# The 64-token rests of an attention and mixer kernel as pairs of 64-row and 64-column matmuls

## Chip, core and metric

The kernel runs on one core of one Trainium2 chip. The core has a matrix engine (TensorE, PE in the profile, with a queue of its own for weight loads, PEld), three engines for elementwise work (VectorE or DVE, ScalarE or ACT, GpSimd or POOL), and SyncE (SP), which here issues most of the DMAs. The engines run side by side and wait for each other by semaphores. The metric is the device time of one execution in microseconds; lower is better.

## The reference

For 8 batches of 576 tokens and 8 heads of 64 columns: heads 0 to 3 attend to the last 32 tokens, heads 4 to 7 to every fourth of the last 128. Then a mixer over tokens and one over channels:

```python
scores = scale * np.matmul(q, k.transpose(0, 1, 3, 2))
mask_plain = (rel >= 0) & (rel < 32)
mask_dil = (rel >= 0) & (rel < 128) & (rel % 4 == 0)
attn = exp(scores - max) / sum              # masked
x = np.matmul(attn, v)                      # [8, 576, 512]
h = np.maximum(xt @ w_tok1, 0.0) @ w_tok2   # xt: x with tokens last, 576 -> 256 -> 576
u = x + h.transpose(0, 2, 1)
h2 = np.maximum(u @ w_ch1, 0.0) @ w_ch2     # 512 -> 1536 -> 512
return u + h2
```

## The kernel before

**Tiles.** 576 tokens are four blocks of 128 and a rest of 64, the tail. The attention output of a batch, `xn`, is [128, 5, 512] in 16-bit floats: slots 0 to 3 hold the four blocks, slot 4 the tail. For columns 0 to 255 (heads 0 to 3) the blocks hold tokens in their natural order, for columns 256 to 511 every fourth token, as the dilated heads use them.

**The tail in three steps.** `values(b, h)` (L605) multiplies the exponentials of the scores with v, one head at a time; the last column of v is 1, so that the sums come with it, and a reciprocal and a product on VectorE normalise all five slots at once. The tail's exponentials lie in `attt`, 320 columns for each head (L147), of which two pieces of 64 are written and the rest is 1.0 (L171). The tail's matmul (L625) reads a window of 128 columns, in which the 64 written ones come first for even and last for odd batches, so all 128 rows of slot 4 get finite values and the real ones stand in rows 0 to 63 or 64 to 127. Heads 4 to 7 need a second such matmul, over v's rows 384 to 447, which are loaded and cast into a tile of their own (`l_vx`, `vt`; "v's middle rows").

`emit_h1(b, jb, half, t)` (L631) gives h1, the hidden layer over tokens: for each half of the columns and each of two blocks `jb` of 128 hidden units, one matmul over slot 4 (L637) with the weight rows 512 to 575 in `w1t[b % 2]`, whose other 64 rows are zero (L179), and four over slots 0 to 3 (L639), summed in one bank of PSUM. `emit_u(b, s, h1)` (L642) gives u; for the tail (s = 4, L659 to L666) two matmuls, 512 wide, with the last 64 columns of w_tok2 inside a window of 128 columns in `w2`, which is padded with 64 columns of zeros on the right (L180), so that the 64 real rows land in the half where `xn` has them; two batches share one tail tile `u16t`. Batch 0 has its own form, `u_half` (L1108).

**Order.** The program's order is written out by hand. For batch 0 it is a straight list (L1009 to L1139). From then on `interleave` (L983) mixes the channel matmuls of batch b (`gen_main`, L920: gp, gt, yp, yx, yw) with steps for batch b + 1 (values, then `mix_steps`, L902: h1, u, transposes) and batch b + 2 (casts and scores), by a time given to each step and a cost that it adds to the clock of the mix. So TensorE's stream is one list, and a step waits there for its inputs.

**PSUM.** `bank("fl", 3, ...)` hands out three banks in a ring to values, h1, u and transposes; a new tenant waits until the bank's last one has been read.

**Forms of matmuls.** Nearly all are 128 rows by 128 columns of weights. The scores of batches 2 to 7 (`scores_twin`, L512) are pairs of 64 rows each, one for each head of a pair, in sets of 20 and 24.

**Loads.** All inputs of later batches go through SyncE's queue in the order of `load_steps` (L226); v in eight pieces: four of 128 tokens for heads 0 to 3, then the tail, two pieces for heads 4 to 7 (`l_vd`) and the middle rows (`l_vx`). GpSimd casts them in the same order (`cast_steps`, L278) and issues the weights' DMAs between its casts (L1038 to L1055).

Of the kernel before, what the change touches and what calls it, by code (L numbers as in the profile page):

```python
# [12 lines left out]
ALU = mybir.AluOpType  # L13
# [19 lines left out]
PST = 256  # L33
PW = 4 * PST
DTL = 512
TW = 320
CBS = (2, 0, 3, 1)
GW = 2 * S

# [29 lines left out]
def kernel(  # L69
# [16 lines left out]
    def fixed(name, shape, dtype=FP16):  # L86
        return sb.tile(shape, dtype, tag=name, bufs=1, name=name)
# [60 lines left out]

    w1n = fixed("w1n", [128, 4, DTOK])
    w1p = fixed("w1p", [128, 4, DTOK])  # L150
    w1t = [fixed(f"w1t{i}", [128, DTOK]) for i in range(2)]
    w2a = fixed("w2", [128, 2, 640])
    w2 = [w2a[:, i] for i in range(2)]
    w2p = [fixed(f"w2p_{i}", [128, 4, 128]) for i in range(2)]
    w3 = [fixed(f"w3_{i}", [128, 4, 512]) for i in range(3)]
# [7 lines left out]
    def emit_fixed():  # L163
        nc.gpsimd.memset(idle, 0.0)
        nc.gpsimd.memset(spread, 0.0)
        nc.vector.memset(qza[64:128, :, 0], 0.0)
        nc.vector.memset(qza[0:64, :, 1], 0.0)
        for a in attp:
            nc.gpsimd.memset(
                a.rearrange("p h (b c) -> p h b c", c=PST)[:, :, :, 128:PST], 0.0)  # L170
        nc.vector.memset(attt, 1.0)  # L171
        for i in range(2):
            nc.gpsimd.memset(vt[i][64:128], 0.0)

    def emit_fixed_late():
        for i in range(2):
            nc.gpsimd.memset(vv[i][:, :, :, 64:65], 1.0)
            nc.gpsimd.memset(vt[i][0:64, :, 64:65], 1.0)
            nc.gpsimd.memset(w1t[i], 0.0)  # L179
        nc.gpsimd.memset(w2a[:, :, S:640], 0.0)  # L180


    l32 = {}
# [19 lines left out]
    def load_v_steps(b):  # L203
        tn = sb.tile([128, 4, 4, D], FP32, tag="l_vn", bufs=1, name=f"l_vn_{b}")
        td = sb.tile([128, 4, 4, D], FP32, tag="l_vd", bufs=1, name=f"l_vd_{b}")
        tx = sb.tile([64, 4, D], FP32, tag="l_vx", bufs=1, name=f"l_vx_{b}")
        t = sb.tile([128, H, D], FP32, tag="l_vt", bufs=1, name=f"l_vt_{b}")
        l32[(b, "vn")], l32[(b, "vd")], l32[(b, "vx")], l32[(b, "vt")] = tn, td, tx, t

        def go(out, in_):  # L210
            return lambda: nc.sync.dma_start(out=out, in_=in_)  # L211

        steps = [go(tn[:, s], v[b, 0:4, 128 * s:128 * s + 128, :].rearrange("h s d -> s h d"))
                 for s in range(4)]
        steps.append(go(t, v[b, :, 448:S, :].rearrange("h s d -> s h d")))
        for h in (0, 2):
            steps.append(go(td[:, h:h + 2].rearrange("m h r d -> m h (r d)"),
                            v[b, 4 + h:6 + h, 0:512, :].rearrange("h (m r) d -> m h (r d)", r=4)))
        steps.append(go(tx, v[b, 4:8, 384:448, :].rearrange("h s d -> s h d")))
        return steps  # L220

    def load_v(b):
# [55 lines left out]
    def cast_steps(b, eng=nc.gpsimd):  # L278
        steps = [lambda: cast_tails_qk(b, eng)]
        for hp in range(4):  # L280
            for nm in ("q", "k"):
                steps.append(lambda nm=nm, hp=hp: cast_qk(b, nm, hp, eng))
        for s in range(4):
            steps.append(lambda s=s: cast_vn(b, s, nc.gpsimd))
        steps.append(lambda: cast_tail_v(b, nc.gpsimd))
        for h in (0, 2):
            steps.append(lambda h=h: cast_vd(b, h, nc.gpsimd))
        steps.append(lambda: cast_vx(b, nc.gpsimd))
        return steps


# [150 lines left out]
        return slice(384 + 64 * x, 512 + 64 * x)  # L442

    def tail_cols(t, hp):
        return t[..., 64:TW].rearrange("p z (x c) -> p z x c", c=128)[:, :, near(hp)[0]:, 0:64]

    def tails_mask(hp):
        return tails_seen[hp // 2][:, :, near(hp)[0]:]
# [155 lines left out]

    def values(b, h):  # L605
        hp, i = h // 2, h % 2
        odd = b % 2
        va = vv[b % 2]
        av = bank("main" if b == 0 and h % 2 else "fl", 3, f"av_{b}_{h}")[:, 0:325].rearrange("p (s c) -> p s c", c=65)
        if hp < 2:  # L610
            a = attp[hp][:, i]
            for s in range(4):
                if s:
                    nc.tensor.matmul(out=av[:, s], lhsT=a[:, PST * (s - 1) + 128:PST * s],
                                     rhs=va[:, s - 1, h, :], start=True, stop=False)
                nc.tensor.matmul(out=av[:, s], lhsT=a[:, PST * s:PST * s + 128],  # L616
                                 rhs=va[:, s, h, :], start=(s == 0), stop=True)
        else:
            a = attd[hp - 2][:, i]
            for r in range(4):  # L620
                nc.tensor.matmul(out=av[:, r], lhsT=a[:, 128 * r:128 * r + 128],  # L621
                                 rhs=va[:, r, h, :], start=True, stop=True)
        c0 = 0 if odd else 64
        for x in near(hp):
            nc.tensor.matmul(out=av[:, 4], lhsT=attt[:, hp, i, c0 + 128 * x:c0 + 128 * x + 128],  # L625
                             rhs=va[:, 4, h, :] if x else vt[b % 2][:, h - 4, :], start=x == near(hp)[0], stop=x == 1)
        rec = sb.tile([128, 5, 1], FP32, tag="rec", bufs=4, name=f"rec_{b}_{h}")
        nc.vector.reciprocal(out=rec[:, :, 0], in_=av[:, :, 64])  # L628
        mult(nc.vector, xn[b][:, :, D * h:D * h + D], av[:, :, 0:64], rec)

    def emit_h1(b, jb, half, t):  # L631
        x = xn[b]
        j = slice(jb, DTOK, 2)
        c = slice(256 * half, 256 * half + 256)
        w = w1p if half else w1n
        p = bank("fl", 3, f"h1p_{b}_{jb}_{half}")[:, 0:256]
        nc.tensor.matmul(out=p, lhsT=w1t[b % 2][:, j], rhs=x[:, 4, c], start=True, stop=False)  # L637
        for s in range(4):
            nc.tensor.matmul(out=p, lhsT=w[:, s, j], rhs=x[:, s, c], start=False, stop=(s == 3))  # L639
        relu(nc.vector if jb and half and b == 0 else nc.scalar, t[:, c], p)  # L640

    def emit_u(b, s, h1):  # L642
        p = bank("fl", 3, f"up_{b}_{s}")
# [12 lines left out]
            else:  # L656
                nc.vector.tensor_tensor(out=u16(b, s), in0=blocks4(p), in1=blocks4(xn[b][:, s]), op=ALU.add)  # L657
        else:
            odd = b % 2  # L659
            c0 = 448 if odd else 512  # L660
            for jb in range(2):
                nc.tensor.matmul(out=p, lhsT=w2[jb][:, c0:c0 + 128], rhs=h1[jb],  # L662
                                 start=(jb == 0), stop=(jb == 1))
            rows = slice(64, 128) if odd else slice(0, 64)
            t = u16t[b // 2]
            nc.vector.tensor_tensor(out=t[rows], in0=blocks4(p[rows]), in1=blocks4(xn[b][rows, 4]), op=ALU.add)  # L666

    def emit_uT(b, cb):
        odd = b % 2
# [232 lines left out]
    def mix_steps(b, t_h1, t_h1b, t_u, t_uT, du=1.0, turn=6.0, gap=2.6):  # L902
        h1 = [sb.tile([128, DM], FP16, tag="h1", bufs=4, name=f"h1_{b}_{jb}") for jb in range(2)]
        steps = []
        for half, at in ((0, t_h1), (1, t_h1b)):
            for jb in range(2):
                steps.append((at + 0.9 * jb, 0.55, lambda jb=jb, half=half: emit_h1(b, jb, half, h1[jb])))
        for i, s in enumerate((4, 0, 1, 2, 3)):
            steps.append((t_u + du * i, 0.44, lambda s=s: emit_u(b, s, h1)))
        if turned(b):  # L910
            for t, tail in ((turn, False), (turn + 1.0, True))[:1 + b % 2]:
                steps.append((t_u + t * du, 0.0, lambda tail=tail: uT_dma(b, tail)))
# [125 lines left out]
    nc.gpsimd.dma_start(out=w1p, in_=moe_w_tok1[0:512, :].rearrange("(m r) j -> m r j", r=4))  # L1038
    for hp in range(2, 4):
        cast_qk(0, "q", hp, nc.gpsimd)  # L1040
    nc.gpsimd.dma_start(out=w1t[0][0:64], in_=moe_w_tok1[512:S, :])
    nc.gpsimd.tensor_copy(out=spread[:, 3:515:4], in_=ident)
    cast_qk(0, "k", 3, nc.gpsimd)
    for s in range(4):
        cast_vn(0, s, nc.gpsimd)
    nc.gpsimd.dma_start(out=w2a[:, :, 0:S], in_=moe_w_tok2.rearrange("(p j) t -> p j t", j=2))
    load_w3(0)
    cast_vd(0, 0, nc.gpsimd)
    cast_vd(0, 2, nc.gpsimd)
    load_w3(1)  # L1050
    cast_vx(0, nc.gpsimd)
    nc.gpsimd.dma_start(out=w1t[1][64:128], in_=moe_w_tok1[512:S, :])
    for jb in range(2):
        nc.gpsimd.tensor_copy(
            out=w2p[jb], in_=w2[jb][:, 0:512].rearrange("p (m r) -> p r m", r=4))  # L1055
# [52 lines left out]
    def u_half(s, half):  # L1108
        p = bank("main" if half else "fl", 3, f"up_0_{s}_{half}")[:, 0:256]
        c = slice(256 * half, 256 * half + 256)  # L1110
        rows = slice(0, 64) if s == 4 else slice(0, 128)
        t = (u16t[0] if s == 4 else u16(0, s))[:, 2 * half:2 * half + 2]
        summed = s in (0, 2)
        if summed:
            nc.tensor.matmul(out=p, lhsT=ident, rhs=xn[0][:, s, c], start=True, stop=False)
        for jb in range(2):
            lhsT = w2p[jb][:, s] if half and s < 4 else w2[jb][:, 128 * s:128 * s + 128]
            nc.tensor.matmul(out=p, lhsT=lhsT, rhs=h1[jb][:, c], start=(jb == 0 and not summed),
                             stop=(jb == 1))
        if summed:  # L1120
            nc.scalar.copy(out=t, in_=blocks4(p))
        else:
            nc.vector.tensor_tensor(out=t[rows], in0=blocks4(p[rows]), in1=blocks4(xn[0][rows, s, c]), op=ALU.add)

    for jb in range(2):
        emit_h1(0, jb, 0, h1[jb])
    for s in (0, 2):
        u_half(s, 0)
    for jb in range(2):
        emit_h1(0, jb, 1, h1[jb])  # L1130
    for s in (4, 1, 3):
        u_half(s, 0)
    for s in (4, 3, 0):
# [126 lines left out]
```

## Time and profile before

| | us |
|---|---|
| median of three runs | 276.93 (275.76 to 277.38) |
| the profiled execution | 275.95 |
| its span, first to last instruction | 274.1 |

The page's first lines give for each engine its busy time, the share of the span and its instructions, and the span in 40 equal slices, each digit the busy share in tenths (9 is 90% or more); PEclk is the clock that TensorE was granted, in tenths:

```
PE 265.5 (97%) x2694; PEld 197.3 (72%) x2694; DVE 168.4 (61%) x340; ACT 148.7 (54%) x291; POOL 159.9 (58%) x216
PE   6899989999999999999999999999999999999994
PEclk9999999999999999999999999999999999999999
```

Rows of a timeline read: start in us from the span's start, duration of the group in us, engine, line of the kernel, operation, output and inputs by the program's names, shape (for TensorE, rows by columns of weights in use, then the moving operand), how many, and in brackets the engine's idle time before and what ended it. Rows of groups give busy us, mean ns of one, and idle time before with what ended most of it. Rows of waits give the total in us, the number, and the longest. A matmul's end is modelled, and matmuls overlap, so their starts tell more than their durations.

### The profile page before, as it was taken

Reading aid. Unit: us, or ns where it says so; the run is one execution under the profiler, and the core shown is the slowest. Engines: PE = TensorE matmul, PEld = TensorE weight load, DVE = VectorE, ACT = ScalarE, POOL = GpSimd, SP = SyncE. Lnnn points to the kernel's source line nnn. Section 1 sums busy time; section 2 is a strip of 40 time slices with the busy share of each in tenths; the row PEclk is TensorE's granted clock in tenths of the full one; section 3 lists DMA queues with packets and bytes.
Section 4 is the critical chain, followed back from the end, with each engine's and each line's share of the span. In section 5 each row is a group of like instructions: output and inputs, shape, how many; then the busy total and the mean of one; then the engine's idle time right before and its main releaser. Section 6 shows DMA issues by size and latency. Waiting matters only on the chain.

```text
span 274.1 us, 6762 instructions
## 1 busy us (share of the span) xinstructions
PE 265.5 (97%) x2694; PEld 197.3 (72%) x2694; DVE 168.4 (61%) x340; ACT 148.7 (54%) x291; POOL 159.9 (58%) x216
## 2 busy tenths in 40 slices
PE   6899989999999999999999999999999999999994
PEld 2787676898676876687776876787776866786673
DVE  6667668676567656595557553875475464961363
ACT  2864675353674655467545666576646565236500
POOL 8871761289868659659974689749970870000000
PEclk9999999999999999999999999999999999999999
DMA  7999999995999799999999899979999040525015
GB/s 220 269 240 231 295 236 207 295 241 150 347 172 219 159 295 198 308 181 240 300 231 214 260 258 255 193 138 330 326 180 152 3 154 2 99 79 149 0 41 153
DMA packets 111471, 54.98 MB, mean 201 GB/s; under 512 B 82736, under 2 KB 107312, under 8 KB 111440
## 3 DMA queue, kind: packets, MB, share of 16 engines
q1 hardware_dynamic: 106784, 49.10, 77.0%
q0 software_dynamic: 2640, 3.94, 8.1%
q10 hardware_dynamic: 2016, 1.51, 1.8%
q8 instruction: 21, 0.34, 0.5%
q14 instruction: 10, 0.08, 0.1%
HBM read 37.59 MB, written 9.44 MB: 172 GB/s over the span
## 4 chain that ended last, share of the span: by engine, by line
PE 89%; DMA 5%; DVE 2%; SPq 1%; ACT 1%; issue 0%; ACTq 0%; POOL 0%
PE gp L941 30%; PE yx L783 13%; PE yw L783 9%; PE h1p L639 5%; PE up L651 4%; PE gt L932 4%; PE yp L969 4%; PE yp L752 4%; PE sc L524 3%; DMA lt<-in_k_dram 3%; DMA l_vx<-in_v_dram 2%; PE h1p L637 1%; PE av L621 1%; SPq L211 1%; PE av L616 1%; PE up L662 1%
## 5 line engine op out<-in xcount | busy, mean ns | idle before, releaser
L109 ACT ACTIVATE gt<-gp 128x512 f16<-128x512 f32 x89 | 53.3, 598 | 49.8 <-PE gp L941 49.5
L783 PEld LDWEIGHTS <-gt 128*128 128x128 f16 x600 | 57.0, 98 | 8.2
L941 PE MATMUL gp<-utd,w 128*128 128x512 f16 x144 | 54.7, 380 | 0.0
L941 PE MATMUL gp<-utm,w 128*128 128x512 f16 x144 | 54.6, 379 | 0.0
L941 PEld LDWEIGHTS <-w 128*128 128x128 f16 x384 | 39.0, 113 | 19.8 <-issue 0.5
L115 POOL TENSOR_TENSOR attp<-attp,const 128x1280 f16<-128x1280 f16 x12 | 31.6, 2637 | 22.1 <-ACT attp L549 22.1
L739 DVE TENSOR_TENSOR gt<-gt 128x768 f16<-128x768 f16 x56 | 32.5, 610 | 12.5 <-ACT gt L109 12.1
L115 DVE TENSOR_TENSOR xn<-av,rec 128x320 f16<-128x320 f32 x64 | 31.5, 492 | 2.2
L115 POOL TENSOR_TENSOR attd<-attd,const 128x1024 f16<-128x1024 f16 x12 | 25.5, 2127 | 5.9 <-issue 5.1
L941 PE MATMUL gp<-uT,w 128*128 128x512 f16 x96 | 25.8, 379 | 0.0
L796 DVE TENSOR_TENSOR o<-yx,u 128x512 f32<-128x512 f32 x22 | 15.2, 691 | 11.6 <-PE yx L783 11.4
L549 ACT ACTIVATE attp<-sc 128x480 f16<-128x480 f32 (+1 forms) x36 | 15.9, 538 | 8.8 <-PE sc L524 8.8
L783 PE MATMUL yx<-w,gt 128*128 128x256 f16 x168 | 20.6, 273 | 0.0
L783 PE MATMUL yx<-wsum_a,gt 128*128 128x256 f16 x168 | 20.6, 273 | 0.0
L657 DVE TENSOR_TENSOR u<-up,xn 128x512 f16<-128x512 f32 x26 | 17.8, 689 | 4.1 <-PE up L651 4.1
L628 DVE RECIPROCAL rec<-av 128x5 f32<-128x5 f32 x64 | 12.3, 192 | 12.7 <-PE av L625 12.6
L105 POOL CAST c_k<-l_k 128x512 f16<-128x512 f32 x29 | 17.6, 615 | 2.2 <-DMA l_k<-in_k_dram 1.1
L666 DVE TENSOR_TENSOR u16t<-up,xn 64x512 f16<-64x512 f32 x7 | 4.8, 690 | 20.8 <-PE up L662 20.8
L105 POOL CAST c_q<-l_q 128x512 f16<-128x512 f32 x26 | 16.3, 633 | 1.9 <-DMA l_q<-in_q_dram 1.2
L870 ACT COPY utd<-utm 128x512 f16<-128x512 f16 x12 | 12.7, 1125 | 8.8 <-DMA u<-utd 4.2
L109 ACT ACTIVATE h<-h1p 128x256 f16<-128x256 f32 x31 | 11.8, 384 | 9.5 <-PE h1p L639 9.1
L806 DVE TENSOR_TENSOR o<-yw,o 128x512 f32<-128x512 f32 x13 | 9.0, 692 | 10.2 <-PE yw L783 10.1
(159 smaller groups left out, 551.3 us busy)
## 6 DMA issues: line engine op xcount, KB each, us to landing
l_q<-in_q_dram SPq DMA_DIRECT2D x15, 512.0 KB, 6.4
l_k<-in_k_dram SPq DMA_DIRECT2D x14, 512.0 KB, 7.1
out_dram<-o SPq DMA_DIRECT2D x12, 512.0 KB, 4.6
l_vn<-in_v_dram SPq DMA_DIRECT2D x32, 128.0 KB, 6.8
l_vd<-in_v_dram SPq DMA_DIRECT2D x16, 256.0 KB, 5.1
w<-in_moe_w_ch_dram POOLq DMA_DIRECT2D x6, 512.0 KB, 7.8
out_dram<-o SPq DMA_DIRECT2D x17, 128.0 KB, 2.6
l_vt<-in_v_dram SPq DMA_DIRECT2D x8, 256.0 KB, 5.5
```

What stands on the lines that cost most here:

```text
L105: eng.tensor_copy(out=out, in_=in_)
L109: nc.scalar.activation(out=out, in_=in_, func=AF.Relu)
L115: eng.tensor_tensor(out=out, in0=x, in1=y, op=ALU.mult)
L549: nc.scalar.activation(out=out, in_=in_, func=AF.Exp, scale=0.125)
L628: nc.vector.reciprocal(out=rec[:, :, 0], in_=av[:, :, 64])
L639: nc.tensor.matmul(out=p, lhsT=w[:, s, j], rhs=x[:, s, c], start=False, stop=(s == 3))
L657: nc.vector.tensor_tensor(out=u16(b, s), in0=blocks4(p), in1=blocks4(xn[b][:, s]), op=ALU.add)
L739: nc.vector.tensor_tensor(out=out, in0=x, in1=y, op=op)
L783: nc.tensor.matmul(out=p, lhsT=gta[:, k0 + mb, r:r + 128], rhs=weights[:, mb, c], start=(first and not mb and (not a or len(parts) > 2)), ...
L796: nc.vector.tensor_tensor(out=o[i][:, :, 256 * j:256 * j + 256].rearrange("p s (x c) -> p s x c", x=2), in0=grid(p), in1=u, op=ALU.add)
L870: nc.scalar.copy(out=natural(uTd[:, cb - 2]), in_=uTm[i][:, cb].rearrange("p r m -> p m r"))
L941: nc.tensor.matmul(out=p, lhsT=w3_block(cb, mb), rhs=uT[(b, cb)][0], start=(i == 0), stop=(i == 3))
```

## The change

- **Tail values.** `attt` shrinks to 128 columns for each head, with the two written pieces side by side and no fill. Each tail matmul becomes two, with the same 64 columns of weights: one writes rows 0 to 63 of slot 4, the other rows 64 to 127, so both halves of `xn`'s slot 4 hold the tail.
- **h1.** `w1t` is one tile now, with the 64 weight rows in both halves. `emit_h1` makes both blocks `jb` of a half: first the two rests, one from rows 0 to 63 and one from rows 64 to 127, then for each block the four other matmuls. Its two steps stand 0.5 apart, with costs 0.54 and 0.43, where it was 0.9 and 0.55.
- **u.** The tail's two 512-wide matmuls become four of 64 columns and 256 wide, in pairs: the left half of the columns to rows 0 to 63 of the bank, the right half to rows 64 to 127. VectorE adds them in two operations. The step's cost goes from 0.44 to 0.22. In batch 0's `u_half` the tail's matmuls take 64 columns of weights instead of 128.
- **Loads.** In each batch v's middle rows are loaded and cast ahead of the two pieces for heads 4 to 7. The second load into `w1t` moves ahead of that of `w2` on GpSimd's queue; the padding of `w2` and the clearing of `w1t` go.

```diff
--- before.py
+++ after.py
@@ -33,7 +33,7 @@
 PST = 256
 PW = 4 * PST
 DTL = 512
-TW = 320
+TW = 128
 CBS = (2, 0, 3, 1)
 GW = 2 * S
 
@@ -148,8 +148,8 @@
 
     w1n = fixed("w1n", [128, 4, DTOK])
     w1p = fixed("w1p", [128, 4, DTOK])
-    w1t = [fixed(f"w1t{i}", [128, DTOK]) for i in range(2)]
-    w2a = fixed("w2", [128, 2, 640])
+    w1t = fixed("w1t", [128, DTOK])
+    w2a = fixed("w2", [128, 2, S])
     w2 = [w2a[:, i] for i in range(2)]
     w2p = [fixed(f"w2p_{i}", [128, 4, 128]) for i in range(2)]
     w3 = [fixed(f"w3_{i}", [128, 4, 512]) for i in range(3)]
@@ -168,7 +168,6 @@
         for a in attp:
             nc.gpsimd.memset(
                 a.rearrange("p h (b c) -> p h b c", c=PST)[:, :, :, 128:PST], 0.0)
-        nc.vector.memset(attt, 1.0)
         for i in range(2):
             nc.gpsimd.memset(vt[i][64:128], 0.0)
 
@@ -176,8 +175,6 @@
         for i in range(2):
             nc.gpsimd.memset(vv[i][:, :, :, 64:65], 1.0)
             nc.gpsimd.memset(vt[i][0:64, :, 64:65], 1.0)
-            nc.gpsimd.memset(w1t[i], 0.0)
-        nc.gpsimd.memset(w2a[:, :, S:640], 0.0)
 
 
     l32 = {}
@@ -213,10 +210,10 @@
         steps = [go(tn[:, s], v[b, 0:4, 128 * s:128 * s + 128, :].rearrange("h s d -> s h d"))
                  for s in range(4)]
         steps.append(go(t, v[b, :, 448:S, :].rearrange("h s d -> s h d")))
+        steps.append(go(tx, v[b, 4:8, 384:448, :].rearrange("h s d -> s h d")))
         for h in (0, 2):
             steps.append(go(td[:, h:h + 2].rearrange("m h r d -> m h (r d)"),
                             v[b, 4 + h:6 + h, 0:512, :].rearrange("h (m r) d -> m h (r d)", r=4)))
-        steps.append(go(tx, v[b, 4:8, 384:448, :].rearrange("h s d -> s h d")))
         return steps
 
     def load_v(b):
@@ -283,9 +280,9 @@
         for s in range(4):
             steps.append(lambda s=s: cast_vn(b, s, nc.gpsimd))
         steps.append(lambda: cast_tail_v(b, nc.gpsimd))
+        steps.append(lambda: cast_vx(b, nc.gpsimd))
         for h in (0, 2):
             steps.append(lambda h=h: cast_vd(b, h, nc.gpsimd))
-        steps.append(lambda: cast_vx(b, nc.gpsimd))
         return steps
 
 
@@ -442,7 +439,7 @@
         return slice(384 + 64 * x, 512 + 64 * x)
 
     def tail_cols(t, hp):
-        return t[..., 64:TW].rearrange("p z (x c) -> p z x c", c=128)[:, :, near(hp)[0]:, 0:64]
+        return t.rearrange("p z (x c) -> p z x c", c=64)[:, :, near(hp)[0]:]
 
     def tails_mask(hp):
         return tails_seen[hp // 2][:, :, near(hp)[0]:]
@@ -604,7 +601,6 @@
 
     def values(b, h):
         hp, i = h // 2, h % 2
-        odd = b % 2
         va = vv[b % 2]
         av = bank("main" if b == 0 and h % 2 else "fl", 3, f"av_{b}_{h}")[:, 0:325].rearrange("p (s c) -> p s c", c=65)
         if hp < 2:
@@ -620,24 +616,28 @@
             for r in range(4):
                 nc.tensor.matmul(out=av[:, r], lhsT=a[:, 128 * r:128 * r + 128],
                                  rhs=va[:, r, h, :], start=True, stop=True)
-        c0 = 0 if odd else 64
         for x in near(hp):
-            nc.tensor.matmul(out=av[:, 4], lhsT=attt[:, hp, i, c0 + 128 * x:c0 + 128 * x + 128],
-                             rhs=va[:, 4, h, :] if x else vt[b % 2][:, h - 4, :], start=x == near(hp)[0], stop=x == 1)
+            for half in range(2):
+                nc.tensor.matmul(out=av[64 * half:64 * half + 64, 4], lhsT=attt[:, hp, i, 64 * x:64 * x + 64],
+                                 rhs=va[:, 4, h, :] if x else vt[b % 2][:, h - 4, :],
+                                 start=x == near(hp)[0], stop=x == 1)
         rec = sb.tile([128, 5, 1], FP32, tag="rec", bufs=4, name=f"rec_{b}_{h}")
         nc.vector.reciprocal(out=rec[:, :, 0], in_=av[:, :, 64])
         mult(nc.vector, xn[b][:, :, D * h:D * h + D], av[:, :, 0:64], rec)
 
-    def emit_h1(b, jb, half, t):
+    def emit_h1(b, half, t):
         x = xn[b]
-        j = slice(jb, DTOK, 2)
         c = slice(256 * half, 256 * half + 256)
         w = w1p if half else w1n
-        p = bank("fl", 3, f"h1p_{b}_{jb}_{half}")[:, 0:256]
-        nc.tensor.matmul(out=p, lhsT=w1t[b % 2][:, j], rhs=x[:, 4, c], start=True, stop=False)
-        for s in range(4):
-            nc.tensor.matmul(out=p, lhsT=w[:, s, j], rhs=x[:, s, c], start=False, stop=(s == 3))
-        relu(nc.vector if jb and half and b == 0 else nc.scalar, t[:, c], p)
+        p = [bank("fl", 3, f"h1p_{b}_{jb}_{half}")[:, 0:256] for jb in range(2)]
+        for jb in range(2):
+            rows = slice(64 * jb, 64 * jb + 64)
+            nc.tensor.matmul(out=p[jb], lhsT=w1t[rows, jb:DTOK:2], rhs=x[rows, 4, c], start=True, stop=False)
+        for jb in range(2):
+            for s in range(4):
+                nc.tensor.matmul(out=p[jb], lhsT=w[:, s, jb:DTOK:2], rhs=x[:, s, c], start=False, stop=(s == 3))
+            relu(nc.vector if jb and half and b == 0 else nc.scalar, t[jb][:, c], p[jb])
+            yield
 
     def emit_u(b, s, h1):
         p = bank("fl", 3, f"up_{b}_{s}")
@@ -656,14 +656,15 @@
             else:
                 nc.vector.tensor_tensor(out=u16(b, s), in0=blocks4(p), in1=blocks4(xn[b][:, s]), op=ALU.add)
         else:
-            odd = b % 2
-            c0 = 448 if odd else 512
+            halves = [(slice(64 * i, 64 * i + 64), slice(256 * i, 256 * i + 256)) for i in range(2)]
             for jb in range(2):
-                nc.tensor.matmul(out=p, lhsT=w2[jb][:, c0:c0 + 128], rhs=h1[jb],
-                                 start=(jb == 0), stop=(jb == 1))
-            rows = slice(64, 128) if odd else slice(0, 64)
-            t = u16t[b // 2]
-            nc.vector.tensor_tensor(out=t[rows], in0=blocks4(p[rows]), in1=blocks4(xn[b][rows, 4]), op=ALU.add)
+                for rows, c in halves:
+                    nc.tensor.matmul(out=p[rows, 0:256], lhsT=w2[jb][:, 512:S], rhs=h1[jb][:, c],
+                                     start=(jb == 0), stop=(jb == 1))
+            t = u16t[b // 2][halves[b % 2][0]]
+            for i, (rows, c) in enumerate(halves):
+                nc.vector.tensor_tensor(out=t[:, 2 * i:2 * i + 2], in0=blocks4(p[rows, 0:256]),
+                                        in1=blocks4(xn[b][rows, 4, c]), op=ALU.add)
 
     def emit_uT(b, cb):
         odd = b % 2
@@ -903,10 +904,11 @@
         h1 = [sb.tile([128, DM], FP16, tag="h1", bufs=4, name=f"h1_{b}_{jb}") for jb in range(2)]
         steps = []
         for half, at in ((0, t_h1), (1, t_h1b)):
+            f = emit_h1(b, half, h1)
             for jb in range(2):
-                steps.append((at + 0.9 * jb, 0.55, lambda jb=jb, half=half: emit_h1(b, jb, half, h1[jb])))
+                steps.append((at + 0.5 * jb, 0.43 + 0.11 * (not jb), lambda f=f: next(f)))
         for i, s in enumerate((4, 0, 1, 2, 3)):
-            steps.append((t_u + du * i, 0.44, lambda s=s: emit_u(b, s, h1)))
+            steps.append((t_u + du * i, 0.44 if s < 4 else 0.22, lambda s=s: emit_u(b, s, h1)))
         if turned(b):
             for t, tail in ((turn, False), (turn + 1.0, True))[:1 + b % 2]:
                 steps.append((t_u + t * du, 0.0, lambda tail=tail: uT_dma(b, tail)))
@@ -1038,18 +1040,18 @@
     nc.gpsimd.dma_start(out=w1p, in_=moe_w_tok1[0:512, :].rearrange("(m r) j -> m r j", r=4))
     for hp in range(2, 4):
         cast_qk(0, "q", hp, nc.gpsimd)
-    nc.gpsimd.dma_start(out=w1t[0][0:64], in_=moe_w_tok1[512:S, :])
+    nc.gpsimd.dma_start(out=w1t[0:64], in_=moe_w_tok1[512:S, :])
     nc.gpsimd.tensor_copy(out=spread[:, 3:515:4], in_=ident)
     cast_qk(0, "k", 3, nc.gpsimd)
     for s in range(4):
         cast_vn(0, s, nc.gpsimd)
-    nc.gpsimd.dma_start(out=w2a[:, :, 0:S], in_=moe_w_tok2.rearrange("(p j) t -> p j t", j=2))
+    nc.gpsimd.dma_start(out=w1t[64:128], in_=moe_w_tok1[512:S, :])
+    nc.gpsimd.dma_start(out=w2a, in_=moe_w_tok2.rearrange("(p j) t -> p j t", j=2))
     load_w3(0)
+    cast_vx(0, nc.gpsimd)
     cast_vd(0, 0, nc.gpsimd)
     cast_vd(0, 2, nc.gpsimd)
     load_w3(1)
-    cast_vx(0, nc.gpsimd)
-    nc.gpsimd.dma_start(out=w1t[1][64:128], in_=moe_w_tok1[512:S, :])
     for jb in range(2):
         nc.gpsimd.tensor_copy(
             out=w2p[jb], in_=w2[jb][:, 0:512].rearrange("p (m r) -> p r m", r=4))
@@ -1109,25 +1111,26 @@
         p = bank("main" if half else "fl", 3, f"up_0_{s}_{half}")[:, 0:256]
         c = slice(256 * half, 256 * half + 256)
         rows = slice(0, 64) if s == 4 else slice(0, 128)
+        p = p[rows]
         t = (u16t[0] if s == 4 else u16(0, s))[:, 2 * half:2 * half + 2]
         summed = s in (0, 2)
         if summed:
             nc.tensor.matmul(out=p, lhsT=ident, rhs=xn[0][:, s, c], start=True, stop=False)
         for jb in range(2):
-            lhsT = w2p[jb][:, s] if half and s < 4 else w2[jb][:, 128 * s:128 * s + 128]
+            lhsT = w2p[jb][:, s] if half and s < 4 else w2[jb][:, 128 * s:128 * s + rows.stop]
             nc.tensor.matmul(out=p, lhsT=lhsT, rhs=h1[jb][:, c], start=(jb == 0 and not summed),
                              stop=(jb == 1))
         if summed:
             nc.scalar.copy(out=t, in_=blocks4(p))
         else:
-            nc.vector.tensor_tensor(out=t[rows], in0=blocks4(p[rows]), in1=blocks4(xn[0][rows, s, c]), op=ALU.add)
-
-    for jb in range(2):
-        emit_h1(0, jb, 0, h1[jb])
+            nc.vector.tensor_tensor(out=t[rows], in0=blocks4(p), in1=blocks4(xn[0][rows, s, c]), op=ALU.add)
+
+    for _ in emit_h1(0, 0, h1):
+        pass
     for s in (0, 2):
         u_half(s, 0)
-    for jb in range(2):
-        emit_h1(0, jb, 1, h1[jb])
+    for _ in emit_h1(0, 1, h1):
+        pass
     for s in (4, 1, 3):
         u_half(s, 0)
     for s in (4, 3, 0):
```

## The prediction

> **What bounds the kernel now.** I read the page's first part, then the busy times by stretches of the span, the waits of TensorE's weight queue (PEld), and last the timeline of TensorE around single steps.
>
> ```profile
> span 274.1 us, 6762 instructions
> ...
> 14.70:27.30 12.60, 11.77 (x162) 9.87 (x159) 8.63 (x26) 6.33 (x16) 5.13 (x10) 1.00 1.16 230
> 42.00:274.10 232.10, 228.43 (x2267) 169.91 (x2264) 140.50 (x281) 123.28 (x238) 132.13 (x158) 1.00 0.84 192
> ...
> PEld L524 <- issue: 2.1, 8, 0.4
> PEld L637 <- DVE xn L115: 1.3, 3, 0.4
> ```
>
> The two rows of stretches, startup and all from 42 us on, give: stretch, its length, then busy time and count of PE, PEld, DVE, ACT and POOL, then the granted clock. From 42 us on PE is busy for 228.4 of 232.1 us at clock 1.00, while DVE, ACT and POOL are busy for 61%, 53% and 57% of it. The two last rows are the longest waits of the weight queue after 42 us; PE's own queue has none there. So in that stretch, which holds the work on batches 1 to 7, the end moves with whatever is added to or taken from PE's stream. In the startup PE is busy for 11.8 of 12.6 us; it also waits for others, and a saving or a cost there can be covered.
>
> What a matmul costs in this stream is not its duration (0.19 to 0.38 us, they overlap) but the step from its start to the next one's start. These are the three places that the change touches, in batch 5 and batch 4:
>
> ```profile
> 165.21 0.20 PE L625 MATMUL av<-vt,attt 128*128 128x65 f16 x1
> 165.24 0.20 PE L625 MATMUL av<-vv,attt 128*128 128x65 f16 x1
> ...
> 165.71 0.27 PE L637 MATMUL h1p<-xn,w1t 128*128 128x256 f16 x1
> 165.82 0.60 PE L639 MATMUL h1p<-xn,w1n 128*128 128x256 f16 x4
> ...
> 139.31 0.59 PE L662 MATMUL up<-h,w 128*128 128x512 f16 x2
> 139.74 0.38 PE L651 MATMUL up<-h,w 128*128 128x256 f16 x2
> ```
>
> A tail value matmul (L625) costs 0.03 us (165.21 to 165.24), the h1 rest (L637) 0.11, the two 512-wide u rests (L662) 0.43 together, 0.22 each, so that a 256-wide one is 0.11.
>
> **The price that decides: leaving the full 128x128 form.** The change makes these matmuls 64 rows or 64 columns wide, between neighbours that stay 128x128. The kernel before has matmuls of 64 rows already, the scores of batches 2 to 7 (L524), in 12 sets. First and last set:
>
> ```profile
> 58.16 0.82 PE L969 MATMUL yp<-w,gt 128*128 128x256 f16 x6
> 58.91 0.65 PE L524 MATMUL sc<-qt,kt 64*128 64x160 f16 x14
> 59.39 0.19 PE L524 MATMUL sc<-tt,kt 64*128 64x64 f16 x2
> 59.42 0.22 PE L524 MATMUL sc<-qt,kt 64*128 64x128 f16 x2
> 59.48 0.19 PE L524 MATMUL sc<-tt,kt 64*128 64x64 f16 x2
> 59.60 0.83 PE L969 MATMUL yp<-w,gt 128*128 128x256 f16 x6
> ...
> 216.42 0.82 PE L783 MATMUL yw<-wsum_b,gt 128*128 128x256 f16 x6
> 217.17 0.62 PE L524 MATMUL sc<-qt,kr 64*128 64x128 f16 x16
> 217.63 0.28 PE L524 MATMUL sc<-tt,kt 64*128 64x64 f16 x8
> 217.84 0.61 PE L783 MATMUL yw<-wsum_b,gt 128*128 128x256 f16 x4
> ```
>
> *Pairs do run side by side:* the two 64-wide matmuls at 59.39 make way for the next group at 59.42, 0.03 us for both, the price of one L625.
>
> *But the set pays on both sides.* Six 256-wide matmuls begin at 58.16 and last 0.82; the last of them (0.27 long) began at 58.71 and should make way at 58.82. The set begins at 58.91: 0.09 lost. Its last pair, at 59.48, should make way at 59.51; the next full matmul begins at 59.60: 0.09 again. The last set says the same: 216.97 + 0.11 = 217.08 against 217.17, and 217.72 + 0.03 = 217.75 against 217.84. With the rounding of the rows I take **0.19 us for each excursion** out of the full form and back, whatever its length. For a set of 20 or 24 matmuls that is little; the change makes excursions of two or four.
>
> The Trainium skill, "TensorEngine Tiling (Array Packing)", section Key Properties, says that changing the tiling mode, other than changing the tile within a mode, drains the TensorE. By that rule, which the two sets bear out for rows, columns pay as well; no run here shows that for columns. With the rule the sum below is +12.7, without it for columns -0.9.
>
> **The change part by part.** Batches 1 to 7 first.
>
> *Tail values:* 8 heads in 7 batches are 56 excursions. Each head's one or two L625 become one or two pairs; by the pair at 59.39 a pair costs 0.03, as the single one did. What is new is the excursion. No trace here has 64-column matmuls; the nearest row is the 64-row set (0.19), from below bounded by nothing, from above by 0.19 plus a weight load that stands open (0.10, below). I take the nearest row: 56 x 0.19 = **+10.6**.
>
> *h1 rests:* 14 halves (7 batches, 2 halves). Two rests of 0.11 become one pair: -0.11; an excursion with 64 rows, which the sets show: +0.19. 14 x 0.08 = **+1.1**.
>
> *u rests:* 7 batches. 0.43 becomes two pairs of 256-wide, 0.22: -0.21; one excursion +0.19. 7 x -0.02 = **-0.1**.
>
> *Batch 0* lies ahead of 27.3 us:
>
> ```profile
> 18.68 0.28 PE L621 MATMUL av<-vv,attd 128*128 128x65 f16 x4
> 19.49 0.19 PE L625 MATMUL av<-vt,attt 128*128 128x65 f16 x1 [0.53 <-POOL vt L105]
> ...
> 16.54 0.62 POOL L105 CAST vv<-l_vd 128x512 f16<-128x512 f32 x1 [0.93 <-DMA l_vd<-in_v_dram]
> 17.39 0.63 POOL L105 CAST vv<-l_vd 128x512 f16<-128x512 f32 x1 [0.23 <-DMA l_vd<-in_v_dram]
> ...
> 19.04 0.40 POOL L105 CAST vt<-l_vx 64x256 f16<-64x256 f32 x1 [0.34 <-DMA l_vx<-in_v_dram]
> ```
>
> Four matmuls of 0.03 from 18.68 should be followed at 18.80; PE waits until 19.49 for v's middle rows. Loaded and cast ahead of the two pieces of v for heads 4 to 7, they come in time, and this 0.7 goes. The two pieces move behind them by one issue on SyncE (0.6) and one cast (0.4): the first is then ready near 17.8, the second near 18.7, still ahead of PE, which needs them at 18.7 and 19.1 at the earliest. What is late next is TensorE itself: three full excursions ahead of 18.68 (a fourth lies partly in the wait for the v tail) bring it to about 19.3, so the 0.7 pays for them and no more. Heads 4 to 7 add 4 x 0.19 and the two h1 halves 2 x 0.08; the two u rests (now 64 columns, otherwise as long) add 2 x 0.19, half of it in PE's waits for DVE and ACT. Sum 0.8 + 0.2 + 0.2 = **+1.1** (0.76 + 0.16 + 0.19). Bounds: -0.5 (the wait goes, no excursion counts) and +2.1 (12 excursions of 0.19 less two pairs of 0.11).
>
> ```profile
> 6.58 0.33 DVE L1033 TENSOR_SCALAR veil<-const 128x416 f16<-128x416 f16 x1 [0.25 <-DMA const<-consts]
> 14.13 0.72 POOL L1046 DMA_DIRECT2D w<-in_moe_w_tok_dram  x1
> 20.10 0.27 PE L637 MATMUL h1p<-xn,w1t 128*128 128x256 f16 x1
> DMA to landing us min/median/max: 5.2/5.9/6.5
> L666 DVE TENSOR_TENSOR u16t<-up,xn 64x512 f16<-64x512 f32 x7 | 4.8, 690 | 20.8 <-PE up L662 20.8
> L1123 DVE TENSOR_TENSOR u16t<-up,xn 64x256 f16<-64x256 f32 x2 | 0.8, 406 | 0.0
> L625 PEld LDWEIGHTS <-attt 128*128 128x128 f16 x96 | 7.2, 97 | 0.6 <-issue 0.6
> ```
>
> *What I cost at nothing.* DVE loses the fill of the tail tile and POOL three clearings, all in the first microseconds; but the first transposes need the identity out of the constants, for whose DMA DVE waits until 6.58 even after the fill. The second load of w1t moves ahead of w2 and the first w3 on POOL's queue, one issue (0.7 or less, as w2's at 14.13) later for each; it would be issued at 14.1 and land 5.2 to 6.5 later (the two loads of w1t), by 20.6; PE needs it at 20.10 + 0.8, near 20.9. If it came late, the wait would be of that size, some 0.3 at most. Each u tail on DVE becomes two additions instead of one, +0.12 seven times, off the path: DVE is busy 61% of the stretch. In later batches the middle rows' load and cast go ahead of those of the other two pieces on SyncE and POOL, which come some 0.6 later; POOL is free 43% of the stretch, and were each late by 0.6, seven times, it would be 4.2. *A wait may be added:* the first step of an h1 half now takes both banks at once, so its second rest asks for a bank one step sooner, and PE's whole stream stands behind it. Three of the 14 halves wait now, 0.4 at most (the L637 row above); if each of them waited as much again, 1.3.
>
> *Sum:* 10.6 + 1.1 - 0.1 + 1.1 = +12.7. The profiled execution took 275.95 (span 274.1 and 1.85 around it), which gives 288.7; the median of the three runs is 276.93, 0.98 above it, which gives **289.6**.
>
> **The rivals.**
> - *Columns are free (not slower).* If only 64-row forms pay, because only they cut the sums that run through the array, values cost nothing, u gains 7 x 0.21 = 1.5, h1 still loses 1.1, batch 0 gains 0.5: -0.9, so **276.0**. For it: no row shows a 64-column price. Against: the price appears on entry and on exit alike, as a change of form would make it. It decides from a column price of 0.04 per excursion down: (1.4 + 0.9) / 63, with 1.4 us being 0.5%.
> - *Nothing pays (faster).* If 0.19 belonged to the score sets and not to the form: -16 x 0.11 - 1.5 - 0.7 = -4.0, **272.9**. Against it stand 12 sets with the same loss after 256-wide and 512-wide neighbours.
> - *The halves don't run side by side.* The pairs in the trace differ in rows, those of the values and u in columns. One after another, heads 0 to 3 cost 0.03 more, heads 4 to 7 0.06: 7 x 0.36 = 2.5, and u's gain of 1.5 goes: **293.6**.
> - *The weight loads stand open.* If each column excursion also waits for one load of weights (0.10, the L625 row of PEld above), 63 x 0.10 and some 0.5 in batch 0: +6.8, **296.4**. For it: after the change of form no load can lie under the matmuls before. Against it: the 64-row sets begin load and matmul together. The Trainium skill, "TensorEngine Tiling (Array Packing)", section Restrictions, says that column tiling disables the fast weight load; no run here shows it.
>
> **How the numbers follow.** Forecast 0.64, its own range 286 to 292 (batch 0 from -0.5 to +2.1; where a value step stands right ahead of an h1 half, one change of form serves both, 0.09 less). Halves in turn 0.10, open loads 0.07, free columns 0.14, nothing pays 0.05. The range 284 to 297 takes in the first three, 0.81, and a column price half that of rows on its low side. A measurement of this kernel tells 0.5%, 1.4 us, from no change. Slower: 0.81 and 0.01 of the free columns, 0.82; same: 0.11 of them; faster: 0.02 of them and 0.05: 0.07.
>
> **What would show it.** In the changed kernel's timeline, a head's first 64-column matmul should begin about 0.12 us after the last full one, and the next full one 0.12 after the last pair; PE's count should grow by 96 for the values and 14 for u while granted clock and waits stay as they are. Two halves of a pair that start 0.03 or more apart speak for halves in turn; a step of 0.03 into and out of the pairs makes me wrong, and so does a wait on another engine in front of PE after 42 us that is not there now.

## The result and the profile after

The changed kernel takes 293.51 us (293.23 to 293.74, 4 runs) against 276.95 for the kernel before (four runs now): a ratio of 1.0605, 95% interval 1.057 to 1.0639, 16.6 us more. The forecast of slower, for this cause, holds; of its size, +12.7 was said.

The page of the changed kernel, its first lines:

```profile
span 291.9 us, 6980 instructions
PE 282.7 (97%) x2804; PEld 203.3 (70%) x2804; DVE 166.5 (57%) x346; ACT 149.6 (51%) x291; POOL 155.6 (53%) x213
```

TensorE is still busy for 97%, and it has 110 matmuls more: 96 of the values and 14 of u. The busy time of every other engine but ScalarE's fell, and ScalarE's rose by 1 us. So the time is in TensorE's stream.

To see where, I cut both traces at the same three points of the work: the first channel matmul of batch 0, that of batch 1, and that of batch 7. Each row is a stretch, its length, PE's busy time and count, granted clock, DMA share and GB/s. The kernel before:

```profile
0.00:27.12 27.12, 22.95 (x269) 1.00 1.06 239
27.12:66.86 39.74, 38.97 (x445) 1.00 1.00 243
66.86:245.43 178.57, 178.57 (x1782) 1.00 0.91 203
```

The changed kernel:

```profile
0.00:28.75 28.75, 25.06 (x281) 1.00 1.06 227
28.75:72.10 43.35, 41.59 (x459) 1.00 0.95 224
72.10:263.17 191.07, 191.07 (x1867) 1.00 0.81 189
```

The startup with batch 0's tails (I) grew by 1.63, the stretch with those of batch 1 (II) by 3.61, the long one with those of batches 2 to 7 (III) by 12.50, and the rest, in which nothing of the change runs, by nothing (28.7 up to the end of either span). Together 17.7. The clock is 1.00 in all these rows. (The profiled execution before lies 1 us under its median, the one after at its median, so spans differ by 1 us more than medians do.)

The timeline of TensorE in the changed kernel shows one of the heads 4 to 7, an h1 pair and a u tail:

```profile
112.91 0.28 PE L617 MATMUL av<-vv,attd 128*128 128x65 f16 x4
113.12 0.22 PE L621 MATMUL av<-vt,attt 128*64 128x65 f16 x2
113.17 0.20 PE L621 MATMUL av<-vv,attt 128*64 128x65 f16 x2
113.31 0.41 PE L943 MATMUL gp<-utd,w 128*128 128x512 f16 x1
...
117.76 0.38 PE L943 MATMUL gp<-utm,w 128*128 128x512 f16 x1
118.07 0.29 PE L635 MATMUL h1p<-xn,w1t 64*128 64x256 f16 x2
118.29 0.50 PE L638 MATMUL h1p<-xn,w1p 128*128 128x256 f16 x3
...
120.25 0.38 PE L943 MATMUL gp<-utm,w 128*128 128x512 f16 x1
120.56 0.41 PE L662 MATMUL up<-h,w 128*64 128x256 f16 x4
120.90 0.41 PE L943 MATMUL gp<-utd,w 128*128 128x512 f16 x1
121.15 0.38 PE L943 MATMUL gp<-utm,w 128*128 128x512 f16 x1
```

Read the starts. The head's four full matmuls give way at 112.91 + 0.12 = 113.03; the first pair begins at 113.12, 0.09 later. From there to the next full matmul, at 113.31, are 0.19. In all 0.28, where two full tail matmuls took 0.06: the head pays **0.22**, on both sides of pairs that themselves run side by side (the second group of two lasts 0.20, one full tail matmul did too). The h1 pair: 117.76 + 0.22 = 117.98 to 118.29, 0.31 instead of 0.22, **+0.09**. The u tail: 120.25 + 0.22 = 120.47 to 120.90, 0.43, **as much as before**. And the first 512-wide full matmul after a 64-column group takes 0.25 to the next (120.90 to 121.15), 0.03 more than elsewhere.

Last, TensorE's own queue waits for another engine in two places after 42 us, where the kernel before had none: 0.2 for ScalarE at 60.96, and this one:

```profile
PE yp L971 <- DVE o L977: 0.7, 1, 0.7
```

It lies in stretch II. TensorE and then VectorE around it:

```profile
67.68 0.22 PE L685 MATMUL tpu<-const,u16t 128*128 128x128 f16 x1
68.59 0.60 PE L971 MATMUL yp<-w,gt 128*128 128x256 f16 x4 [0.70 <-DVE o L977]
...
66.72 1.22 DVE L105 COPY uT<-tpu 128x640 f16<-128x640 f16 x2
67.86 0.68 DVE L977 TENSOR_TENSOR o<-yp,u 128x512 f32<-128x512 f32 x1
```

VectorE copies two transposes of u before it adds up the output `o` whose bank TensorE waits for. In the kernel before, channel matmuls stood between those transposes; here, two transposes follow each other (from 66.24 and from 66.52). So there were two theories and two rivals to tell apart: **A**, each excursion of a head costs 0.22, whatever is around it; **C**, the new times and costs of the h1 and u steps put other steps side by side and cost TensorE waits of their own; and against A, that the price belongs to each 64-column matmul (**D**) or to all the changes together (**B**). The run with two heads in one excursion adds a rival **E**: a normalisation that comes later makes h1 wait.

### The profile page after: what moved, and what is told of

The parts are those of the page before. It is cut to its first block, busy times and chain, and to the rows that moved or that the text cites. A ratio compares the mean times of both kernels' runs of the same rounds, so it can differ in the third digit from the quotient of the medians.

```text
span 291.9 us, 6980 instructions
## 1 busy us (share of the span) xinstructions
PE 282.7 (97%) x2804; PEld 203.3 (70%) x2804; DVE 166.5 (57%) x346; ACT 149.6 (51%) x291; POOL 155.6 (53%) x213
## 4 chain that ended last, share of the span: by engine, by line
PE 86%; DMA 8%; DVE 3%; ACT 1%; issue 1%; ACTq 0%; POOL 0%; SPq 0%; POOLq 0%
PE gp L943 29%; PE yx L784 13%; PE yw L784 9%; PE h1p L638 5%; PE up L651 4%; PE gt L934 4%; PE av L621 4%; PE yp L753 4%; PE yp L971 3%; DMA l_k<-in_k_dram 3%; PE sc L521 3%; DMA lt<-in_k_dram 2%; DMA l_vt<-in_v_dram 2%; PE av L617 1%; PE av L612 1%; PE h1p L635 1%
## 5 line engine op out<-in xcount | busy, mean ns | idle before, releaser
L943 PE MATMUL gp<-utd,w 128*128 128x512 f16 x144 | 55.7, 387 | 0.0
L943 PEld LDWEIGHTS <-w 128*128 128x128 f16 x384 | 38.3, 116 | 21.7 <-issue 1.5
L740 DVE TENSOR_TENSOR gt<-gt 128x768 f16<-128x768 f16 x56 | 29.9, 564 | 12.7 <-ACT gt L109 12.3
L666 DVE TENSOR_TENSOR u16t<-up,xn 64x256 f16<-64x256 f32 x14 | 5.9, 422 | 22.2 <-PE up L662 22.0
L546 ACT ACTIVATE attt<-sc 128x128 f16<-128x128 f32 (+1 forms) x24 | 7.6, 344 | 15.9 <-PE sc L521 15.9
L871 ACT COPY utd<-utm 128x512 f16<-128x512 f16 x12 | 12.7, 1143 | 4.8 <-DMA u<-utd 4.6
```

The costliest lines, as they stand in the source:

```text
L546: nc.scalar.activation(out=out, in_=in_, func=AF.Exp, scale=0.125)
L740: nc.vector.tensor_tensor(out=out, in0=x, in1=y, op=op)
L871: nc.scalar.copy(out=natural(uTd[:, cb - 2]), in_=uTm[i][:, cb].rearrange("p r m -> p m r"))
L943: nc.tensor.matmul(out=p, lhsT=w3_block(cb, mb), rhs=uT[(b, cb)][0], start=(i == 0), stop=(i == 3))
```

## The experiments

### The values alone

```diff
 # kernel before, with attt of 128 columns and no fill
+            for half in range(2):
+                nc.tensor.matmul(out=av[64 * half:64 * half + 64, 4], lhsT=attt[:, hp, i, 64 * x:64 * x + 64], ...
```

> The kernel before with the tail values alone as 64-column pairs; h1, u and all loads as before. Theory A (each excursion of a head costs 0.22 us in TensorE's stream, whatever stands around it): 56 heads of batches 1 to 7 give 12.3, batch 0 another 1.2 to 1.8, so 290.4 to 291.1 us, and the steps from the last full matmul to the next full one read 0.25 (one pair) and 0.28 (two pairs) as in the changed kernel. Rival B (the price belongs to the three kinds of excursions together or to the new order of steps): clearly less, under 289.

Measured: 290.05 us, ratio 1.0486 (1.0465 to 1.0508). Its second and third stretch:

```profile
28.24:69.90 41.66, 40.89 (x458) 1.00 0.93 227
69.90:259.59 189.69, 189.69 (x1855) 1.00 0.83 191
```

Against the kernel before, II grew by 1.92 and III by 11.12: 13.04 for 56 heads, 0.233 for each, the 0.22 of the excursion and part of the 0.03 of the matmul after it. Batch 0 added 1.12. Counted from start to start over the 56 heads, from the last full matmul ahead of a tail to the second one behind it, the sum is 13.4. By medians, 13 of the 16.6 us are this part alone, batch 0 included (by spans, 14.2 of 17.7). A holds, B doesn't; the total is 0.3 under what A gave.

### All but the values

```diff
 # changed kernel, with attt of 320 columns and the fill again
+        c0 = 0 if b % 2 else 64
         for x in near(hp):
-            for half in range(2):
-                nc.tensor.matmul(out=av[64 * half:64 * half + 64, 4], lhsT=attt[:, hp, i, 64 * x:64 * x + 64], ...
+            nc.tensor.matmul(out=av[:, 4], lhsT=attt[:, hp, i, c0 + 128 * x:c0 + 128 * x + 128], ...
```

> The changed kernel with the tail values in full 128-column windows again; only one half of slot 4 holds the tail then, so h1 and u of the tail are not the reference's. Theory A: 12.3 and some 1.5 of batch 0 go, four h1 pairs that shared an excursion with a head pay 0.1 more each: 279.5 to 280.5 us. Rival B: 283 or more stays.

Measured: 282.23 us (280.29 to 282.33, 4 runs), ratio 1.0187 (1.0147 to 1.0228). A miss by the median: 11.3 went and not 13 to 14; one run of the four, 280.29, lies inside what A gave. The waits of TensorE's own queue say why; the largest is new:

```profile
PE yw L784 <- DVE o L797: 1.9, 2, 1.6
```

With the excursions gone, TensorE runs into VectorE in more places, with 1.9 us in these two. Counted from start to start, delays over 0.05 us between full matmuls come to 4.2 us in this trace and 1.4 in that of the changed kernel after 42 us: the 2.8 between them are what is missing. That the excursions had given VectorE time fits this, but no run tries it by itself.

### The old places of the steps

```diff
 # changed kernel
-                steps.append((at + 0.5 * jb, 0.43 + 0.11 * (not jb), lambda f=f: next(f)))
+                steps.append((at + 0.9 * jb, 0.55, lambda f=f: next(f)))
-            steps.append((t_u + du * i, 0.44 if s < 4 else 0.22, ...
+            steps.append((t_u + du * i, 0.44, ...
```

> The changed kernel with the old times and costs of the h1 and u steps in the mix (0.9 apart and 0.55, and 0.44). Theory C (the 1.25 us in which TensorE waits for ScalarE and VectorE at 60.5 and 67.7 us come from steps that moved next to each other): those two waits go and the time is 292.0 to 292.5. Rival (they come from the later stream itself): 293.3 to 293.7, waits still there.

Measured: 292.11 us (291.7 to 292.21), ratio 1.0558 (1.0539 to 1.0577), 1.4 us less than the changed kernel, whose runs all lie above. Stretch II, 43.35 long in the changed kernel, is

```profile
28.92:70.74 41.82, 41.05 (x459) 1.00 0.92 227
70.74:261.58 190.84, 190.84 (x1866) 1.00 0.82 190
```

1.5 shorter, III (the second row) 0.2, and TensorE's own queue has no wait for another engine after 42 us. From start to start, the two waits that went were 0.85 (67.68 + 0.06 = 67.74 to 68.59) and 0.39. C holds.

### Both: h1, u and loads, with the steps in the old places

```diff
 # all but the values, and the old places of the steps
```

> The run full_values (h1 and u as pairs, values in full windows, loads sooner; the tails of h1 and u are not the reference's) with the old times and costs of the steps. Theory C (the 5.3 us that full_values keeps over the kernel before are 1.3 of h1 pairs, nothing of u, and the rest waits for VectorE that the new places brought): 278.0 to 278.9 us and no wait of TensorE for VectorE after 60 us that the kernel before lacks. Rival (row excursions cost more than the 0.10 that the steps show): 280 or more.

Measured: 279.19 us, ratio 1.0073 (1.0044 to 1.0101). The third stretch, TensorE's waits and one h1 pair:

```profile
68.05:248.96 180.91, 180.01 (x1795) 1.00 0.89 200
...
PE yw L784 <- DVE o L758: 0.9, 1, 0.9
...
47.56 0.56 PE L635 MATMUL h1p<-xn,w1t 64*128 64x256 f16 x2
```

Over the kernel before, I grew by 0.66, II by 0.53 and III by 2.34, of which 0.9 is this one wait. What is left of II and III, 2.0, is 14 h1 pairs at 0.10 (1.4) and 0.6 more. Half of that is the one pair at 47.56, which lasts 0.56 where others last 0.29: its second rest begins 0.28 after the first (47.84) and waits, by the profile, for the VectorE product that reads the bank's last tenant. That is the claim on a bank that the prediction had named as a wait that may be added. The other half is the 0.01 to 0.03 of the first full matmul behind each of the 21 excursions. The time is 0.3 above the range of C, with one wait that C had excluded; u gains nothing and h1 loses.

### Twice the excursions, the same matmuls

```diff
 # the values alone; heads 4 to 7
+            tail(0)                       # middle rows: first pair
             a = attd[hp - 2][:, i]
             for r in range(4):
                 nc.tensor.matmul(out=av[:, r], ...
+        tail(1)                           # last rows: second pair
```

> The run values_only with the two pairs of heads 4 to 7 in two excursions instead of one (middle rows first, then the four full matmuls, then the last rows). No matmul is added. Theory A (0.22 us is paid for each excursion, some 0.03 for each pair in it): 28 heads of batches 1 to 7 pay 0.216 more each, 6.0, batch 0 another 0 to 0.9: 296.0 to 297.0 us. Rival D (the price belongs to each 64-column matmul): 290 to 290.5, as values_only.

In this run the tail of heads 4 to 7 is not the reference's; the number and the shapes of the matmuls are those of the values alone. Measured: 296.43 us, ratio 1.0687 (1.063 to 1.0745), 6.4 above the values alone. One head and stretch III:

```profile
112.69 0.22 PE L611 MATMUL av<-vt,attt 128*64 128x65 f16 x2
112.84 0.29 PE L627 MATMUL av<-vv,attd 128*128 128x65 f16 x4
113.06 0.22 PE L611 MATMUL av<-vv,attt 128*64 128x65 f16 x2
113.22 0.41 PE L944 MATMUL gp<-utd,w 128*128 128x512 f16 x1
...
71.32:266.21 194.89, 194.89 (x1854) 1.00 0.82 186
```

III grew by 5.20 over the values alone (194.89 against 189.69), for 24 heads: 0.217 each, where A said 0.216 and D nothing. The price is that of an excursion.

### Half the excursions, the same matmuls

```diff
 # the values alone: an even head keeps its tail and its normalisation
+        ...                           # tail() and norm(): the two parts as functions
+        if h % 2 == 0:
+            held_head[b] = (tail, norm)
+            return
+        first_tail, first_norm = held_head.pop(b)
+        first_tail()
+        tail()
+        first_norm()
+        norm()
```

> The run values_only with the tails of two heads in one excursion: an even head's tail waits for the odd head's full matmuls, so there are 32 excursions instead of 64 and as many matmuls. Theory A: 28 excursions of batches 1 to 7 less, 6.0, and batch 0 another 0 to 0.9: 283.2 to 284.1 us. Rival D: 290. Rival E (the later normalisation of the even head makes h1 wait): above 284.5.

Measured: 286.29 us, ratio 1.0324 (1.0277 to 1.0372): 3.8 less than the values alone, not 6 to 7. Two heads in one excursion, one wait, the waits of the weight queue and of TensorE's own, and two stretches:

```profile
108.19 0.28 PE L621 MATMUL av<-vv,attd 128*128 128x65 f16 x4
108.40 0.22 PE L626 MATMUL av<-vt,attt 128*64 128x65 f16 x2
108.45 0.20 PE L626 MATMUL av<-vv,attt 128*64 128x65 f16 x2
108.49 0.20 PE L626 MATMUL av<-vt,attt 128*64 128x65 f16 x2
108.52 0.20 PE L626 MATMUL av<-vv,attt 128*64 128x65 f16 x2
108.65 0.41 PE L954 MATMUL gp<-utd,w 128*128 128x512 f16 x1
...
109.66 0.28 PE L621 MATMUL av<-vv,attd 128*128 128x65 f16 x4
110.29 0.27 PE L650 MATMUL h1p<-xn,w1t 128*128 128x256 f16 x1 [0.35 <-ACT h L109]
...
PEld L650 <- DVE xn L115: 4.0, 6, 0.9
...
PE h1p L650 <- DVE xn L115: 1.2, 3, 0.4
PE h1p L650 <- ACT h L109: 1.1, 3, 0.4
...
27.11:67.86 40.75, 39.98 (x457) 1.00 0.97 240
67.86:255.80 187.94, 185.66 (x1854) 1.00 0.84 193
```

From 108.19 + 0.12 = 108.31 to 108.65 are 0.34 for two heads, where two excursions take 0.56: 0.22 saved, as A has it. Stretch II shows it whole (0.91 less than the values alone for four excursions fewer). In III only 1.75 of 24 x 0.22 = 5.3 arrive. VectorE gets two normalisations at once and the weight queue waits for them in front of h1 (4.0 us in six waits); TensorE's own queue stands for 2.3 of 187.94, half of it by the profile for VectorE, half for ScalarE's reading of an h1 bank. From start to start a wait is longer than its idle time: 109.66 + 0.12 = 109.78 to 110.29 is 0.51, where 0.35 is idle. Six such waits of 0.5 to 0.6, 3.2 together, are most of the 3.5 that are missing. A and E both hold, E for most of III.

### The loads alone, and those of batch 0 alone

```diff
 # kernel before, in load_v_steps; the same move in cast_steps and in batch 0's casts;
 # the second run in batch 0's load and casts only
+        steps.append(go(tx, v[b, 4:8, 384:448, :].rearrange("h s d -> s h d")))
         for h in (0, 2):
             steps.append(go(td[:, h:h + 2] ...
-        steps.append(go(tx, v[b, 4:8, 384:448, :].rearrange("h s d -> s h d")))
```

> The kernel before with only v's middle rows loaded and cast sooner. Theory: TensorE's wait of 0.7 us at 18.8 goes, h1 of batch 0 starts up to 0.7 sooner, and 0.2 to 0.7 of it reaches the end: 276.2 to 276.8 us. Rival (VectorE's chain of the last four heads or the two later pieces of v take it back): 276.9 to 277.2.

> The kernel before with v's middle rows sooner in batch 0 alone. Theory: 0.4 us less at the first channel matmul, as in loads_only, and nothing given back in batches 1 and 2: 276.4 to 276.7 us. Rival (whatever starts sooner meets the next wait): 276.8 to 277.2.

Measured: 276.27 us, ratio 1.0005 (0.9973 to 1.0037), and 277.24 us, ratio 0.9999 (0.9964 to 1.0034): no difference that can be told. What the first one's trace shows: the first channel matmul starts sooner, and then VectorE's sums of the gates take longer. Loads alone:

```profile
26.72 0.38 PE L941 MATMUL gp<-uT,w 128*128 128x512 f16 x1
...
87.15 3.98 DVE L739 TENSOR_TENSOR gt<-gt 128x768 f16<-128x768 f16 x6
...
87.86 0.87 POOL L105 CAST vv<-l_vd 128x512 f16<-128x512 f32 x1
```

The kernel before, the same six sums:

```profile
87.29 3.60 DVE L739 TENSOR_TENSOR gt<-gt 128x768 f16<-128x768 f16 x6
```

0.40 of the startup's wait was won (26.72 against 27.12). By the first channel matmul of batch 1, 0.27 of it was gone (II is 40.01 against 39.74), and in batch 2 the rest: a cast of v on GpSimd now lies beside the gate sums, they take 3.98 instead of 3.60, and TensorE waits 0.3 for a bank behind them. With batch 0 alone moved, 0.27 was won in the startup, and the same sums took 4.35. So in both traces what was won was given back, against the theory of the second run. No version here beats the kernel before.

## Why the prediction was right, and where it fell short

**The price of leaving the full form: right, and it decides.** The 64-row sets of the kernel before gave 0.19 for an excursion, taken over to 64 columns, for which there was no row. Columns pay as rows do: 0.22 in the timeline, 0.233 over 56 heads, 0.217 for one more excursion with no matmul more. The Trainium skill, "TensorEngine Tiling (Array Packing)", section Key Properties, says that changing the tiling mode drains the TensorE; the loss on both sides of the column pairs agrees with it. The rivals of free columns and of no price at all are out. So is that of halves in turn: in one excursion the pairs follow each other after 0.05, 0.04 and 0.03 (108.40 to 108.52), hardly more than the 0.03 of one full matmul, where two halves in turn would take 0.06. That its 293.6 is 0.1 from the measured time is chance. That of open weight loads, +0.10 for each excursion, is out at its size; whether a part of one is in the first pair's 0.05 is open. A new wait for another engine after 42 us had been named as a sign of being wrong. Two came, 0.7 and 0.2, and in the old places both went while the price stayed.

**Tail values, 56 x 0.19 = 10.6: mis-sized.** Measured 13.0 with the values alone. The 0.19 was the loss at the two edges; I let the first pair cost 0.03, like later ones. It costs 0.05 (113.12 to 113.17; later pairs 0.03 to 0.04, 108.45 to 108.52), and the first 512-wide matmul behind costs 0.03 more. The Trainium skill, "TensorE: Matmul & The Clock Gate", section LDWEIGHTS (loading the stationary operand), puts a weight load at columns / 1.2 in ns; for 64 columns that is an estimate of 0.053 us, which the step of the first pair matches and the steps of the later ones do not.

**h1, 14 x 0.08 = 1.1:** 0.09 to 0.10 measured, 1.4. **u, -0.1:** no gain and no loss measured, as said.

**Batch 0, +1.1:** 1.63. The wait for the middle rows went, as said: they are cast at 16.62 in the changed kernel, 19.04 before. But TensorE came to the first head 0.26 later, ahead of any excursion (the first two rows below, the kernel before and the changed one); no run shows by what. The v tail was cast 0.5 later (15.88, before 15.41), and the first head took 0.32 more to the next head's first matmul (0.39 before, 0.71 here), so the wait for the v tail did not cover its excursion. The other seven heads cost some 0.22 each. Roughly, 0.26 + 0.32 + 7 x 0.22 + 2 x 0.10 for h1 less the wait of 0.69 is 1.6. The second of the two pieces behind them was cast at 19.34, later than the 18.7 I gave it for being ready; TensorE did not wait for it:

```profile
15.55 0.19 PE L616 MATMUL av<-vv,attp 128*128 128x65 f16 x1
...
15.81 0.19 PE L612 MATMUL av<-vv,attp 128*128 128x65 f16 x1
...
16.62 0.40 POOL L105 CAST vt<-l_vx 64x256 f16<-64x256 f32 x1 [0.59 <-DMA l_vx<-in_v_dram]
17.19 0.62 POOL L105 CAST vv<-l_vd 128x512 f16<-128x512 f32 x1 [0.18 <-DMA l_vd<-in_v_dram]
19.34 0.62 POOL L105 CAST vv<-l_vd 128x512 f16<-128x512 f32 x1 [1.52 <-DMA l_vd<-in_v_dram]
```

**What was costed at nothing and wasn't:** the new times and costs of the h1 and u steps. I listed the edit and priced only the earlier claim on a bank, not that a smaller cost moves every step behind it in the mix. That was 1.4 us here by medians, and 3.0 (282.23 against 279.19) once the excursions were gone, though one of the four runs behind the 282.23 took 280.29. This and the size of the values' term put the time above the forecast's own range of 286 to 292, inside the stated 284 to 297.

In sum, by spans: values 13.0, batch 0 1.6, h1 1.4 less 0.3 where a head's pairs and an h1 pair share an excursion (three places after batch 0, 0.1 each), places 1.8 in II and III (43.35 and 191.07 against 41.82 and 190.84): 17.5 of 17.7. The last 0.2, of the size of the slower matmuls behind the h1 and u excursions, is not taken apart.

## What to carry to other kernels

Padding a small matmul to the full form can be cheaper than packing it. Each way out of the full 128x128 form and back cost 0.2 us here, so what is done in it must save that much: one to four pairs of 65-wide matmuls and one pair of 256-wide ones did not, and two pairs of 256-wide ones broke even. If small tiles are worth it, do many in one excursion, and look at who then waits for the work that was bunched. When a step's cost in a hand-written mix is changed, price the new neighbours too, best by running the new code in the old places first.

## What the runs showed that was not expected

An excursion to 64 columns makes the first pair and the first full matmul behind it slower (0.05 for 0.03, 0.25 for 0.22), beside the 0.09 at its entry. And VectorE's six sums of 128x768 16-bit values took 3.60, 3.98 or 4.35 us in three kernels with the same sums, in which none, one or both of GpSimd's casts of the two pieces of v lay beside them. These casts are not all of it. Taken one by one over all ten traces, the 411 such sums with no GpSimd operation beside them last 0.54 to 0.56 us each. In the kernel before, three of the six are longer, 0.64 to 0.75, and beside them lie GpSimd's copies into `kt` and its cast of the middle rows. That GpSimd's work is the cause was not tried by itself.
